# Attention and a softplus feed-forward: the first product of the last three token groups in seven block products

## The chip, the core and the metric

The kernel runs on one core of one Trainium2 chip. A core has five engines that run side by side, each through its own list of instructions in order: TensorE (PE in the profile; its weight loads are listed apart as PEld), VectorE (DVE), ScalarE (ACT), GpSimd (POOL) and SyncE (SP), which issues most transfers. They wait for each other through semaphores. TensorE writes its results to PSUM, eight banks of 128 partitions x 512 float32; VectorE and ScalarE read them from there. The metric is the device time of one execution in microseconds (us).

## The reference

Masked attention over 4 sequences of 768 tokens and 8 heads of 64, then a feed-forward layer without biases over all 3072 tokens:

```python
scores = scale * np.matmul(q, k.transpose(0, 1, 3, 2))
scores = np.where(keep, scores + bias, -1e9)      # 96 local keys and 8 global ones, linear bias by distance
a = softmax(scores)
x = np.matmul(a, v)                               # -> [3072, 512] after joining the heads
...
h = x @ w_in                                      # [512, 2048]
g = np.maximum(h, 0.0) + np.log1p(np.exp(-np.abs(h)))   # softplus
return g @ w_out                                  # [2048, 512]
```

## The kernel before

Tokens go in blocks of 128; two blocks make a group of 256, so there are 24 blocks (n = 0 to 23) and 12 groups (g = 0 to 11). A block's attention is: scores on TensorE (`sc`), bias added on VectorE (`z`), exponential on ScalarE (`ex`), the product with v on TensorE (`pv`, in two halves), the normalisation on VectorE (`nm`: a reciprocal and a multiplication), and a transpose by DMA (`xt`) into the group's tile XT. Copies of the global keys and values (`gk`, `gv`) and conversions to bf16 (`castq`, `castk`, `castv`) run on VectorE, ScalarE or POOL.

A group's first feed-forward product is eight steps `a g.p` (function `mm1`): each makes 256 rows of h for 256 tokens, with eight matmuls (4 parts of the 512 inputs x 2 blocks of rows; the weights are 128 x 128 of w_in, 256 columns of XT move), into one of two banks, h0 and h1. ScalarE then takes exp of the bank (`e g.p`, line 1075), and per two steps ln(1 + .) of 1024 columns (`ln g.i`, line 1086), which together are the softplus. The two `e` and one `ln` cover a quarter i of the 2048 rows.

The second product of the groups from 2 on is already done by a scheme with seven block products in place of eight (function `products`, steps `b g.j`, j = 1 to 7, eight matmuls of 256 columns each, line 521): sums of g are made beforehand (`ka g.j`, function `token_sums`, line 451), sums of w_out once (`ws`), and VectorE or ScalarE combines the products in the output tile (`oe g.*`, lines 482 to 504). For groups 2 to 9 products share banks in a chain (`CHAIN`), for 10 and 11 they have banks of their own. `st` stores a result.

What runs when is written out: the list `ORDER` holds every step with its engine (P, V, A, G for POOL, S), and the program issues the steps in just that order; so each engine's list is the part of `ORDER` with its letter. A step's dependences (class `Program`) only decide what it waits for. One instruction at the start loads ScalarE's function table with exp and ln (`table`, line 343).

## Time and profile before

| | |
|---|---|
| median of 3 runs | 210.53 us (209.85 to 210.83) |
| profiled execution | 210.08 us, of which the span from first to last instruction 208.3 us |
| granted TensorE clock | 0.997 of full speed |
| TensorE busy | 201.5 us (97%), 2211 matmuls |
| VectorE busy | 159.8 us (77%) |
| ScalarE busy | 169.0 us (81%) |
| POOL busy | 112.8 us (54%) |

A row of the profile names the line of the kernel, engine, operation, output <- inputs (buffer numbers left out), shapes and the number of instructions. In the view by groups the busy time, the mean duration of one in ns and the idle time ahead of them with its releasers follow; in the timeline a row begins with start and duration in us. A matmul's record runs until its result is drained, so records of following matmuls overlap; how far they really are apart is read from their starts.

### The profile page before, as it was taken

The page shows a single profiled execution, that of the slowest core. Times are in us where ns is not written, and L with a number is a line of the kernel's source. Part 1 is how long each engine was busy: PE and PEld are TensorE (multiplying, and loading weights), DVE is VectorE, ACT ScalarE, POOL GpSimd, SP SyncE. Part 2 cuts the span into 40 slices and gives each one's busy share as a digit, 9 for nine tenths or more (in the row PEclk, how much of TensorE's full clock was granted, in tenths as well). Part 3 has the DMA queues.
Part 4 walks back from the last instruction along what each step waited for, and adds up shares of the span by engine and source line. Part 5 has one row for each costly group of instructions (what it writes and reads, how often), then busy time and mean ns, then how long its engine had stood idle before and what let it go on. Part 6 is the DMA issues. An engine that isn't in the chain of part 4 may idle for free.

```text
span 208.3 us, 5515 instructions
## 1 busy us (share of the span) xinstructions
PE 201.5 (97%) x2211; PEld 164.8 (79%) x2211; DVE 159.8 (77%) x296; ACT 169.0 (81%) x240; POOL 112.8 (54%) x127
## 2 busy tenths in 40 slices
...
GB/s 175 364 361 388 387 358 361 332 245 249 201 271 214 257 210 312 172 188 296 195 212 259 191 200 221 145 152 102 106 73 62 92 5 142 63 0 0 104 22 181
DMA packets 70650, 40.99 MB, mean 197 GB/s; under 512 B 30433, under 2 KB 62689, under 8 KB 70625
## 3 DMA queue, kind: packets, MB, share of 16 engines
...
## 4 chain that ended last, share of the span: by engine, by line
PE 85%; DMA 8%; DVE 2%; POOL 2%; issue 1%; ACTq 0%; ACT 0%; POOLq 0%; DVEq 0%
PE h_ps L1060 38%; PE o_ps L521 25%; PE s_ps L950 5%; PE x_ps L1002 4%; PE s_ps L1107 3%; DMA raw<-in_q_dram 3%; DMA kT<-kb 3%; DMA XT<-xs 2%; PE x_ps L1235 2%; PE x_ps L521 2%; PE s_ps L521 1%; PE s_ps L810 1%; POOL vb L706 1%; PE o_ps L1107 1%; PE o_ps L1002 1%
## 5 line engine op out<-in xcount | busy, mean ns | idle before, releaser
L1060 PE MATMUL h_ps<-XT,w_in_bf 128*128 128x256 bf16 x768 | 94.4, 273 | 0.1
L1060 PEld LDWEIGHTS <-w_in_bf 128*128 128x128 bf16 x768 | 73.2, 98 | 11.0 <-DMA XT<-xs 0.3
L1075 ACT ACTIVATE e<-h_ps 128x512 f32<-128x512 f32 x96 | 60.1, 637 | 17.6 <-PE h_ps L1060 16.6
L1086 ACT ACTIVATE g<-e 128x1024 bf16<-128x1024 f32 x48 | 49.8, 1053 | 0.6
L976 DVE TENSOR_TENSOR z<-s_ps,biasA 128x1024 f32<-128x1024 f32 x38 | 45.9, 1218 | 3.5 <-PE s_ps L950 3.1
L983 ACT ACTIVATE pb<-z 128x1024 bf16<-128x1024 f32 (+1 forms) x44 | 43.4, 993 | 1.3 <-DVE z L976 0.6
L451 POOL TENSOR_TENSOR g<-g 128x1024 bf16<-128x1024 bf16 x11 | 23.9, 2171 | 23.7 <-DVE raw L451 23.5
L521 PEld LDWEIGHTS <-g 128*128 128x128 bf16 x320 | 30.9, 98 | 3.6
L451 POOL TENSOR_TENSOR raw<-g 128x1024 bf16<-128x1024 bf16 x9 | 19.6, 2177 | 15.0 <-ACT g L1086 13.5
L868 POOL COPY vb<-vb 4x512 bf16<-4x512 bf16 x22 | 14.9, 675 | 20.9 <-PE x_ps L1002 16.2
L706 POOL CAST vb<-raw 64x512 bf16<-64x512 f32 x32 | 21.6, 678 | 6.0 <-DMA raw<-in_v_dram 4.7
L521 PEld LDWEIGHTS <-raw 128*128 128x128 bf16 x240 | 22.6, 98 | 2.8
L521 PE MATMUL o_ps<-raw,raw 128*128 128x256 bf16 x192 | 24.3, 273 | 0.0
L451 DVE TENSOR_TENSOR raw<-g 128x1024 bf16<-128x1024 bf16 x21 | 17.2, 829 | 6.5 <-ACT g L1086 4.1
L521 PE MATMUL o_ps<-raw,g 128*128 128x256 bf16 x160 | 19.6, 273 | 0.0
L1002 PEld LDWEIGHTS <-pb 128*128 128x128 bf16 x352 | 16.4, 98 | 3.6 <-ACT pb L983 0.6
L1014 DVE TENSOR_TENSOR xs<-x_ps,rcp 128x256 bf16<-128x256 f32 x40 | 17.0, 424 | 1.4
L1002 PE MATMUL x_ps<-vb,pb 128*128 128x65 bf16 x304 | 15.8, 193 | 0.0
L521 PE MATMUL o_ps<-w_out_bf,g 128*128 128x256 bf16 x128 | 15.8, 273 | 0.0
L1235 PE MATMUL x_ps<-blank 128*128 128x512 bf16 x35 | 11.7, 454 | 1.2 <-DVE blank L1159 1.2
L1013 DVE RECIPROCAL rcp<-x_ps 128x4 f32<-128x4 f32 x40 | 7.1, 178 | 7.4 <-PE x_ps L1002 6.8
L674 POOL CAST qb<-raw 128x1024 bf16<-128x1024 f32 (+1 forms) x9 | 9.3, 1032 | 5.9 <-DMA raw<-in_q_dram 5.6
...
## 6 DMA issues: line engine op xcount, KB each, us to landing
...
```

What stands on the lines that cost most here:

```text
L451: (nc.vector if eng == "DVE" else nc.gpsimd).tensor_tensor(dst, a[0], b[0], ALU.subtract)
L521: nc.tensor.matmul(psum(j), lhs[:, f // 2, f % 2, :], w(f), start=(f == 0 and not (chain and j in "267")), stop=(f == 7), skip_group_check ...
L706: copy_on[eng](dst, src)
L868: copy_on[eng](vb_of(prev)[sl, :, 0:D], vb_of(first)[sl, :, 0:D])
L976: nc.vector.tensor_tensor(z, src, bias, ALU.add)
L983: nc.scalar.activation(pb[:, 0:nr, :].rearrange("p (y a) b -> p y (a b)", y=2), src, AF.Exp, scale=1.0 / root_d)
L1002: nc.tensor.matmul(xv[:, h, :], pb[:, 4 * (h % 2) + 2 * part + h // 2 if lone else u_all * (2 * (h % 2) + h // 2) + u, :], vb_of(prev if u ...
L1014: nc.vector.tensor_tensor(xs[:, 4 * part : 4 * part + 4, :], xv[:, :, 0:D], rcp[:][:, :, None].to_broadcast([P, 4, D]), ALU.mult,)
L1060: last = nc.tensor.matmul(hv[:, j, :], w_in_bf[:, m, fb * P : fb * P + P], XT[g % NXG][:, m, :], start=(m == 0), stop=(m == NM - 1),)
L1075: nc.scalar.activation(e[:, p % 2, :, :].rearrange("p j (b t r) -> p (j b) r t", b=2, r=2), hb[:].rearrange("p (a r t) -> p a r t", a=4, r=2),
L1086: nc.scalar.activation(gt[:, 2 * p - 2 : 2 * p + 2, :].rearrange("p a t -> p (a t)"), e[:].rearrange("p a j t -> p (a j t)"), AF.Ln, bias=1.0,
L1235: nc.tensor.matmul(x_ps[:], blank[:, 0:P], blank[:])
```

## The change

The first product of groups 9, 10 and 11 goes by seven block products as well (`mm1_seven`). Per quarter i of the rows there are four parts on TensorE, in one bank: `mA` (product 1, four matmuls), `mB` (3 and 4, eight), `mC` (5 and 2) and `mD` (7 and 6), each matmul with 128 x 128 weights and 128 columns moving, 28 in all. In between the bank is read: `my` copies product 1 out (ScalarE or VectorE), `mt` adds the two halves of the bank to the copy (VectorE, two instructions), `eo` takes the activation of half of the results straight from the bank (ScalarE), `md` subtracts the bank from the sum (VectorE), and `ed` takes the activation of that (ScalarE). The products 5, 2, 7 and 6 are accumulated onto what stands in the bank, so each part waits for the reading before it. Group 9 uses the banks h0 and h1 in turn; groups 10 and 11 use those and two more (t0, t1), halves of the two score tiles.

Sums of w_in are made once (`kw`, ten instructions of 1024 bf16 columns, six on VectorE and four on POOL), sums of x per group (`kx`, five of 256 columns, mostly on POOL). Group 9 keeps exp and ln (`eo`, `ed`, and `ln` over 1024 columns); groups 10 and 11 take softplus in one activation each, after one more table load, which follows the last `ln` of group 9. The outputs of groups 10 and 11 join the chain form, group 11 with single additions at the end. From the first `ln4.1` on the list `ORDER` is new; ahead of it it is the same. Six token sums `ka` more are on VectorE, and four more first copies of an output (`oe g.a`) are on ScalarE.

ScalarE's list around the first product of group 9, before (line 1075 is exp of a bank, 1086 ln, 983 the attention's exp, 855 and 868 copies of global keys and values):

```order
L1075 ACTIVATE e_104<-h_ps_64 128x4x2x64
L1086 ACTIVATE g_109<-e_106 128x1024
L1075 ACTIVATE e_105<-h_ps_64 128x4x2x64
L983 ACTIVATE pb_100<-z_94 128x1024
L855 COPY kT_88<-kTa_92 128x2x4x2 x2
L983 ACTIVATE pb_99<-z_96 128x1024
L868 COPY vb<-vb 4x8x64
L1075 ACTIVATE e_106<-h_ps_64 128x4x2x64
L1075 ACTIVATE e_104<-h_ps_65 128x4x2x64
L1086 ACTIVATE g_107<-e_104 128x1024
L983 ACTIVATE pb_97<-z_95 128x1024
L1075 ACTIVATE e_105<-h_ps_65 128x4x2x64
```

and now (1204 `my`, 1015 the attention's exp, 1181 `eo` and `ed`, 1267 and 1188 ln, 501 the first copy of an output):

```order
L1204 COPY raw_76<-h_ps_65 128x256
L1204 COPY raw_75<-h_ps_64 128x256
L1015 ACTIVATE pb_97<-z_95 128x1024
L1015 ACTIVATE pb_98<-z_96 128x1024
L887 COPY kT_89<-kTa_92 128x2x4x2 x2
L1181 ACTIVATE e_105<-h_ps_65 128x512
L1181 ACTIVATE e_104<-h_ps_64 128x512
L1267 ACTIVATE g_109<-e_106 128x1024
L1181 ACTIVATE e_105<-raw_76 128x512
L1204 COPY raw_76<-h_ps_65 128x256
L1188 ACTIVATE g_107<-e_105 128x1024
L501 COPY osb_111<-o_ps 128x512
```

Two exp and one ln per quarter became a copy, an exp from the bank, an exp from VectorE's result and an ln, so ScalarE's list now waits for VectorE inside a quarter.

VectorE's list at the same place, before (1013 and 1014 normalise, 976 adds the bias, 451 is a token sum, 485 to 498 combine outputs):

```order
L498 TENSOR_TENSOR osb_111<-osb_111,o_ps 128x2x256
L976 TENSOR_TENSOR z_96<-s_ps_62,biasA 128x1024
L1013 RECIPROCAL rcp_115<-x_ps 128x4
L1014 TENSOR_TENSOR xs_101<-x_ps,rcp_115 128x256
L451 TENSOR_TENSOR raw_79<-g_109 128x1024
L1013 RECIPROCAL rcp_112<-x_ps 128x4
L1014 TENSOR_TENSOR xs_102<-x_ps,rcp_112 128x256
L451 TENSOR_TENSOR g_109<-g_109 128x4x2x128
L485 TENSOR_TENSOR osb_110<-osb_110,o_ps 128x2x256
L976 TENSOR_TENSOR z_94<-s_ps_61,biasA 128x1024
L868 COPY vb<-vb 4x8x64 x2
L976 TENSOR_TENSOR z_95<-s_ps_62,biasA 128x1024
```

and now (1191 and 1192 are `mt`, 1195 `md`, 1204 `my`, 1045 and 1046 normalise, 470 is a token sum, 900 a copy of global values):

```order
L1191 TENSOR_TENSOR raw_76<-raw_76,h_ps_65 128x256
L1192 TENSOR_TENSOR raw_76<-raw_76,h_ps_65 128x256
L1191 TENSOR_TENSOR raw_75<-raw_75,h_ps_64 128x256
L1192 TENSOR_TENSOR raw_75<-raw_75,h_ps_64 128x256
L470 TENSOR_TENSOR raw_78<-g_108 128x1024
L1045 RECIPROCAL rcp_115<-x_ps 128x4
L1046 TENSOR_TENSOR xs_101<-x_ps,rcp_115 128x256
L1195 TENSOR_TENSOR raw_76<-raw_76,h_ps_65 128x512
L900 COPY vb<-vb 4x8x64
L470 TENSOR_TENSOR raw_78<-g_108 128x1024
L1195 TENSOR_TENSOR raw_75<-raw_75,h_ps_64 128x512
L1045 RECIPROCAL rcp_112<-x_ps 128x4
```

Between attention steps VectorE now has the two additions and the subtraction for each quarter, on which `mC`, `ed` and the next user of the bank wait.

ScalarE's list where the softplus of group 9 ends and that of group 10 begins, before (1075 exp of a bank, 1086 ln):

```order
L1086 ACTIVATE g_107<-e_104 128x1024
L1075 ACTIVATE e_106<-h_ps_65 128x4x2x64
L1075 ACTIVATE e_106<-h_ps_64 128x4x2x64
L1075 ACTIVATE e_104<-h_ps_65 128x4x2x64
L1075 ACTIVATE e_104<-h_ps_64 128x4x2x64
L1086 ACTIVATE g_108<-e_105 128x1024
L1075 ACTIVATE e_105<-h_ps_65 128x4x2x64
L1075 ACTIVATE e_105<-h_ps_64 128x4x2x64
L1086 ACTIVATE g_108<-e_106 128x1024
```

and now (359 is the table load, 501 the first copy of an output):

```order
L1188 ACTIVATE g_107<-e_106 128x1024
L1204 COPY e_106<-h_ps_65 128x256
L1181 ACTIVATE e_104<-raw_76 128x512
L1188 ACTIVATE g_107<-e_104 128x1024
L359 ACT_TABLE_LOAD
L501 COPY osb_110<-o_ps 128x512
L1181 ACTIVATE g_108<-h_ps_65 128x512
L1181 ACTIVATE g_108<-h_ps_64 128x512
L1181 ACTIVATE g_108<-s_ps_61 128x512
L1204 COPY e_105<-s_ps_62 128x256
L1181 ACTIVATE g_108<-e_105 128x512
L1181 ACTIVATE g_108<-e_104 128x512
```

From the table load on there is no ln; each half quarter is one activation from a bank (h_ps, s_ps) or from VectorE's result (e).

The diff, cut to its core (of the list `ORDER` one line that was taken out and two that came in):

```diff
     def in_order(self):
 
+        wants = [o for o in (self.ops[name] for name in self.placed) if o.table]
+        for o, p in zip(wants, wants[1:]):
+            if p.table != o.table:
+                o.then = p.table
...
-a8.6:P oe7.a:V gv20.0:G trq11:S castv11.00:V a8.7:P e8.6:A ka7.7:V ex20.0:A sc21.0:P trk11.1:S ka7.5:V b7.1:P e8.7:A
...
+kw6.0:G xt20:S pv21.0:P e8.7:A b6.7:P z22.1:V ln8.2:A st5.1.0:S mA9.0:P mA9.1:P b6.6:P kx9.7:G my9.1:A nm21.0:V
...
+my9.0:A ex22.0:A mB9.1:P ka7.2:G oe6.7:V mB9.0:P mt9.1:V ex22.1:A st6.1.0:S b7.3:P st6.0.0:S mt9.0:V mC9.1:P gk23:A
...
-CHAIN = range(FIRST_S, 10)
+CHAIN = range(FIRST_S, 12)
+APART = (11,)
 S_KEYS = {
-    10: {"3": ("o",), "4": ("o",), "5": ("x",), "2": ("x",), "1": ("s", 0, 0), "7": ("s", 1, 0), "6": ("s", 1, 0)},
-    11: {"3": ("o",), "4": ("o",), "5": ("x",), "2": ("x",), "1": ("s", 0, 0), "7": ("s", 1, 0), "6": ("h0",)},
+    11: {"3": ("x",), "4": ("x",), "1": ("s", 0, 0), "5": ("o",), "7": ("o",), "2": ("s", 1, 0), "6": ("s", 1, 0)},
 }
...
+EXP_TABLE, SOFT_TABLE = "natural_log_exp_and_others", "softplus"
+MM1S = (9, 10, 11)
+MM1_SOFT = (10, 11)
+SOFT = set()
...
+        if key[0][0] == "t":
+            return s_ps[int(key[0][1])][:, 1, :]
...
+        if g in MM1S:
+            view = g_t[g % NGB][:].rearrange("p a t -> p (a t)").rearrange("p (i q f t) -> p i q f t", i=4, q=4, f=2)
+            return view[:, :, {(1, 0): 0, (0, 1): 1, (0, 0): 2, (1, 1): 3}[tb, kh], :, :]
...
+                if g in APART:
+                    if j in "52":
+                        out_op(j, sub_one(j, "52".index(j)), [both["52".index(j)]], j, at + 1, 0.42)
+                    if j in "76":
+                        c = "76".index(j)
+                        out_op(j, add_one(j, c), [ok[c, c]], j, at + 1, 0.42)
+                    continue
...
+    WIN_SUM, b_homes, td_slots = {}, [], []
+
+    def win_part(F, K, h):
+        view = w_in_bf[:, 2 * K : 2 * K + 2, :].rearrange("p m (i k c) -> p m i k c", i=4, k=2)
+        return view[:, :, 2 * h : 2 * h + 2, F, :], [("win", 2 * i + K) for i in (2 * h, 2 * h + 1)]
+
+    def win_sums(rank):
+
+        slots = [idle.popleft() for _ in range(5)]
+        td_slots.extend(idle.popleft() for _ in range(2))
+        for z, (j, a, b, fn) in enumerate((
+            ("1", (0, 0), (1, 1), ALU.add),
+            ("5", (0, 0), (0, 1), ALU.add),
+            ("2", (1, 0), (1, 1), ALU.add),
+            ("7", (1, 1), (0, 1), ALU.subtract),
+            ("6", (0, 0), (1, 0), ALU.subtract),
+        )):
+            for h in range(2):
+                (x, xk), (y, yk) = win_part(*a, h), win_part(*b, h)
+                dst = raw_t[slots[z]].bitcast(BF16)[:, 1024 * h : 1024 * h + 1024]
+                dst = dst.rearrange("p (m i c) -> p m i c", m=2, i=2)
+                WIN_SUM[j, h] = dst
+
+                def ex(eng, dst=dst, x=x, y=y, fn=fn):
+                    (nc.vector if eng == "DVE" else nc.gpsimd).tensor_tensor(dst, x, y, fn)
+
+                op(f"kw{j}.{h}", "DVE", 0.0, rank, ex, reads=xk + yk, writes=[("WI", j, h)], port=True,
+                   after=users(("raw", slots[z], h)), alts={"DVE": 0.64, "POOL": 2.15})
+        for x in range(2):
+            for t, key in ((qb[x], "qb"), (kb[x], "kb")):
+                flat = t[:].rearrange("p a h d -> p (a h d)")
+                for part in range(4):
+                    b_homes.append((flat[:, W * part : W * part + W].rearrange("p (m t) -> p m t", m=2), (key, x, part)))
+
+    def mm1_seven(g, rank):
+        if not WIN_SUM:
+            win_sums(rank - 8.0)
+        B = {(kh, tb): XT[g % NXG][:, 2 * kh : 2 * kh + 2, P * tb : P * tb + P] for kh in range(2) for tb in range(2)}
+        bk = [("XT", 2 * (g % NXG) + tb) for tb in range(2)]
+        moving = {"2": (B[0, 0], bk[:1]), "5": (B[1, 1], bk[1:])}
+        for z, (j, a, b, fn) in enumerate((
+            ("3", (0, 1), (1, 1), ALU.subtract),
+            ("4", (1, 0), (0, 0), ALU.subtract),
+            ("1", (0, 0), (1, 1), ALU.add),
+            ("7", (1, 0), (1, 1), ALU.add),
+            ("6", (0, 0), (0, 1), ALU.add),
+        )):
+            dst, key = b_homes[(5 * (g - MM1S[0]) + z) % len(b_homes)]
+
+            def ex(eng, dst=dst, a=a, b=b, fn=fn):
+                (nc.vector if eng == "DVE" else nc.gpsimd).tensor_tensor(dst, B[a], B[b], fn)
+
+            op(f"kx{g}.{j}", "DVE", 0.0, rank, ex, reads=bk[a[1] : a[1] + 1] + bk[b[1] : b[1] + 1], writes=[key],
+               port=True, alts={"DVE": 0.25, "POOL": 0.6})
+            moving[j] = dst, [key]
+
+        def still(j, i):
+            if j in "34":
+                x, keys = win_part(*((0, 0) if j == "3" else (1, 1)), i // 2)
+                return x[:, :, i % 2, :], keys
+            return WIN_SUM[j, i // 2][:, :, i % 2, :], [("WI", j, i // 2)]
+
+        view = g_t[g % NGB][:].rearrange("p a t -> p (a t)").rearrange("p (i c) -> p i c", i=4)
+
+        for i in range(4):
+            n = 4 * (g - MM1S[0]) + i
+            soft = g in MM1_SOFT
+            ring_x = (("h0",), ("h1",), ("t0",), ("t1",)) if soft else (("h0",), ("h1",))
+            xkey = ring_x[n % len(ring_x)]
+            X = bank(xkey)
+            slot = n % NE
+            e = e_t[slot][:].rearrange("p a j t -> p (a j t)")
+            if soft:
+                td, tk, dk = e, ("e", slot, 0), ("e", slot, 1)
+            else:
+                z = td_slots[n % 2]
+                td, (tk, dk) = raw_t[z][:], raw_keys(z)
+            T, D_ = td[:, 0:W], td[:, 512:1024]
+            at = {j: X[:, 0:W] if j in "1357" else X[:, W:] for j in "1345276"}
+
+            def part(js, i=i, at=at):
+                def fn():
+                    for j in js:
+                        w, b = still(j, i)[0], moving[j][0]
+                        for f in range(2):
+                            for m in range(2):
+                                nc.tensor.matmul(
+                                    at[j][:, P * f : P * f + P], w[:, m, P * f : P * f + P], b[:, m, :],
+                                    start=f == m == 0 and j in "13", stop=m == 1, skip_group_check=True,
+                                )
+
+                return fn
+
+            def needs(js, i=i):
+                return sum((still(j, i)[1] + moving[j][1] for j in js), [])
+
+            def act(src, dst, fn, **kw):
+                def run():
+                    nc.scalar.activation(
+                        dst.rearrange("p (a t r) -> p a t r", a=4, r=2), src.rearrange("p (a r t) -> p a t r", a=4, r=2), fn
+                    )
+
+                return run
+
+            def log(i=i, e=e):
+                nc.scalar.activation(view[:, i, :], e, AF.Ln, bias=1.0)
+
+            def begin(X=X, T=T):
+                nc.vector.tensor_tensor(T, T, X[:, 0:W], ALU.add)
+                nc.vector.tensor_tensor(T, T, X[:, W:], ALU.add)
+
+            def end(X=X, T=T, D_=D_):
+                nc.vector.tensor_tensor(
+                    D_.rearrange("p (a c) -> p a c", a=2), T[:, None, :].to_broadcast([P, 2, W]),
+                    X.rearrange("p (a c) -> p a c", a=2), ALU.subtract,
+                )
+
+            first = users(("s", int(xkey[0][1]))) if xkey[0][0] == "t" and xkey not in pl.writer else []
+            r = rank + 4.0 * i
+            gk = {q: [("g", g % NGB, i, tb, kh) for tb, kh in c] for q, c in ((0, ((1, 0), (0, 1))), (1, ((0, 0), (1, 1))))}
+            op(f"mA{g}.{i}", "PE", 0.22, r, part("1"), reads=needs("1"), writes=[xkey], after=first, count=4)
+            op(f"my{g}.{i}", "ACT", 0.4, r + 0.3, lambda eng, X=X, T=T: copy_on[eng](T, X[:, 0:W]), reads=[xkey], writes=[tk],
+               alts={"ACT": 0.4, "DVE": 0.42})
+            op(f"mB{g}.{i}", "PE", 0.45, r + 0.6, part("34"), reads=needs("34"), writes=[xkey], count=8)
+            op(f"mt{g}.{i}", "DVE", 0.75, r + 0.8, begin, reads=[xkey], writes=[tk], count=2)
+            op(f"mC{g}.{i}", "PE", 0.45, r + 1.0, part("52"), reads=needs("52"), writes=[xkey], count=8)
+            outs = [view[:, i, 512 * q : 512 * q + 512] if soft else e[:, 512 * q : 512 * q + 512] for q in range(2)]
+            ok = [gk[q] if soft else [("e", slot, q)] for q in range(2)]
+            how = dict(table=SOFT_TABLE if soft else EXP_TABLE)
+            fn = AF.Softplus if soft else AF.Exp
+            op(f"eo{g}.{i}", "ACT", 0.64, r + 1.5, act(X, outs[0], fn), reads=[xkey], writes=ok[0], **how)
+            op(f"mD{g}.{i}", "PE", 0.45, r + 2.0, part("76"), reads=needs("76"), writes=[xkey], count=8)
+            op(f"md{g}.{i}", "DVE", 0.69, r + 2.5, end, reads=[xkey, tk], writes=[dk])
+            op(f"ed{g}.{i}", "ACT", 0.64, r + 3.2, act(D_, outs[1], fn), reads=[dk], writes=ok[1], **how)
+            if not soft:
+                op(f"ln{g}.{i}", "ACT", 0.99, r + 3.9, log, reads=ok[0] + ok[1], writes=gk[0] + gk[1], **how)
...
-            mm1(g, p, rank)
+            if g not in MM1S:
+                mm1(g, p, rank)
+        if g in MM1S:
+            mm1_seven(g, 16.0 * g)
...
+        if o.then:
+            table(o.then)
```

113 lines of the change are left out of this document (66 added, 47 removed).

## The prediction

> **What bounds the kernel now.** I read the page's busy times and the chain that ended last, then the busy times by stretch, then the instructions in order of time near the end.
>
> ```profile
> PE 201.5 (97%) x2211; PEld 164.8 (79%) x2211; DVE 159.8 (77%) x296; ACT 169.0 (81%) x240; POOL 112.8 (54%) x127
> ...
> PE 85%; DMA 8%; DVE 2%; POOL 2%; issue 1%; ACTq 0%; ACT 0%; POOLq 0%; DVEq 0%
> ```
>
> TensorE is busy 97% of the span and holds 85% of the chain. A busy PE could still be waiting inside a record, so the next view matters more (busy us of PE, PEld, DVE, ACT, POOL, then clock, DMA share, GB/s, for three stretches of 36 us).
>
> ```profile
> 30.00:66.00 36.00, 35.79 (x374) 25.06 (x372) 33.42 (x58) 34.12 (x47) 19.96 (x28) 1.00 1.16 267
> 113.00:149.00 36.00, 36.00 (x420) 31.81 (x417) 27.38 (x48) 31.35 (x45) 25.84 (x23) 1.00 0.86 170
> 149.00:185.00 36.00, 36.00 (x409) 31.78 (x407) 24.83 (x42) 29.62 (x43) 14.97 (x11) 1.00 0.26 67
> ```
>
> The second half, where the order is new, has no idle PE at all at full clock; VectorE stands at 76% and 69%, ScalarE at 87% and 82%. The timeline says the same in single steps:
>
> ```profile
> 187.05 1.91 PE L1060 MATMUL h_ps<-XT,w_in_bf 128*128 128x256 bf16 x16
> ...
> 188.79 1.91 PE L521 MATMUL o_ps<-raw,raw 128*128 128x256 bf16 x16
> ...
> 190.54 1.91 PE L1060 MATMUL h_ps<-XT,w_in_bf 128*128 128x256 bf16 x16
> ...
> 200.05 0.68 DVE L492 TENSOR_TENSOR osb<-osb,s_ps 128x512 f32<-128x512 f32 x1
> ...
> 200.65 0.68 DVE L482 COPY osb<-o_ps 128x512 f32<-128x512 f32 x1
> ...
> 203.68 1.04 PE L521 MATMUL h_ps<-raw,raw 128*128 128x256 bf16 x8
> 204.31 0.42 DVE L504 TENSOR_TENSOR osb<-osb,s_ps 128x256 f32<-128x256 f32 x1
> 204.75 0.42 DVE L504 TENSOR_TENSOR osb<-osb,h_ps 128x256 f32<-128x256 f32 x1
> ```
>
> Sixteen matmuls over 256 columns start 1.745 us before the next sixteen, 0.109 us each, whatever product they belong to. (VectorE's steps overlap a little when one follows the other: 200.05 to 200.65, 0.60 for a record of 0.68.) So the stage is worth what leaves TensorE's queue, less every wait that newly appears in it. Time saved on ScalarE alone is worth nothing here.
>
> **The change part by part.** *TensorE.* Each of the groups 9, 10, 11 loses 64 matmuls over 256 columns and gains 4 x 28 = 112 over 128 columns, each with its own weight load. Rows with that shape exist early in the kernel, and 65-column ones everywhere:
>
> ```profile
> 22.90 0.61 PE L810 MATMUL s_ps<-ident_p,qb 128*128 128x128 bf16 x8
> 23.35 0.61 PE L810 MATMUL s_ps<-ident_p,kb 128*128 128x128 bf16 x8
> 23.79 0.41 PE L1002 MATMUL o_ps<-vb,pb 128*128 128x65 bf16 x8
> ...
> 175.34 0.39 PEld L1002 LDWEIGHTS <-pb 128*128 128x128 bf16 x8
> 175.45 0.41 PE L1002 MATMUL x_ps<-vb,pb 128*128 128x65 bf16 x8
> 175.65 0.63 ACT L1075 ACTIVATE e<-h_ps 128x512 f32<-128x512 f32 x1 [0.23 <-PE h_ps L1060]
> ...
> 175.69 1.91 PE L1060 MATMUL h_ps<-XT,w_in_bf 128*128 128x256 bf16 x16
> ...
> 175.90 0.18 DVE L1013 RECIPROCAL rcp<-x_ps 128x4 f32<-128x4 f32 x1 [1.30 <-PE x_ps L1002]
> ```
>
> Sixteen of 128 columns take 23.79 - 22.90 = 0.89 us, 0.0556 each; eight of 65 columns with a full weight load each take 0.24 us, 0.03 each, so weight loads are hidden well below 128 columns. Removed: 192 x 0.109 = 20.9 us. Added: 336 x 0.0556 = 18.7 us. That is **-2.2 us**. The lower end is -2.5 (0.053, from 23.35 to 23.79 rounded down), the upper end is +11.9 (192 x 0.109 against 336 x 0.098, a weight load's record, if each load stood in the open); I take the 128-column row, which is the same shape.
>
> A rule of the Trainium skill speaks against this part: in "TensorE: Matmul & The Clock Gate", section "Back-to-back issue gap", a stream of load-and-multiply pairs is put at about 81 ns each at 128 columns. By that figure the added work would be 336 x 0.081 = 27.2 us and the sum of this part +6.3 us, an estimate from that page. The rows above disagree with it.
>
> *The new waits.* A block product's quarter passes one PSUM bank four times: product 1; a copy out (my); products 3 and 4; two additions (mt); 5 and 2; an activation (eo); 7 and 6; a subtraction (md). Each step needs the one before, through another engine. Durations (busy, mean ns):
>
> ```profile
> L1075 ACT ACTIVATE e<-h_ps 128x512 f32<-128x512 f32 x96 | 60.1, 637 | 17.6 <-PE h_ps L1060 16.6
> L1086 ACT ACTIVATE g<-e 128x1024 bf16<-128x1024 f32 x48 | 49.8, 1053 | 0.6
> ...
> L451 DVE TENSOR_TENSOR raw<-g 128x1024 bf16<-128x1024 bf16 x21 | 17.2, 829 | 6.5 <-ACT g L1086 4.1 <-PE o_ps L521 2.4
> L1014 DVE TENSOR_TENSOR xs<-x_ps,rcp 128x256 bf16<-128x256 f32 x40 | 17.0, 424 | 1.4
> ...
> L451 DVE TENSOR_TENSOR g<-g 128x1024 bf16<-128x1024 bf16 x9 | 6.2, 686 | 0.0
> ...
> L868 DVE COPY vb<-vb 4x512 bf16<-4x512 bf16 x7 | 3.5, 496 | 0.1
> L482 ACT COPY osb<-o_ps 128x512 f32<-128x512 f32 x5 | 2.9, 582 | 3.8 <-PE o_ps L521 3.8
> ...
> L492 DVE TENSOR_TENSOR osb<-osb,s_ps 128x512 f32<-128x512 f32 x2 | 1.4, 680 | 0.0
> L343 ACT ACT_TABLE_LOAD x1 | 1.3, 1283 | 1.5 <-PEq L1372 1.5
> ...
> L1211 ACT ACTIVATE biasA<-raw 128x256 bf16<-128x256 f32 x2 | 0.7, 408 | 0.0
> L488 DVE TENSOR_TENSOR osb<-osb,x_ps 128x256 f32<-128x256 f32 x2 | 0.8, 422 | 2.7 <-ACT osb L482 2.5 <-PE x_ps L521 0.2
> ```
>
> my is 0.4 (L1211, 256 columns); mt two of L488, 0.77 as they overlap; a bf16 sum (ka, kw) 0.69 (L451, g<-g), 0.6 behind another; eo 0.64; md 0.68 (L492). From PE taking up its next work to the reader's start there are 0.2 us (175.45 to 175.65 for ScalarE, 175.69 to 175.90 for VectorE). Back to PE it is 0.05; the row after that is a score product's step in the chain, 0.55:
>
> ```profile
> 14.61 1.09 ACT L817 COPY kTa<-s_ps 128x512 bf16<-128x512 bf16 x2
> ...
> 15.75 0.41 PE L950 MATMUL s_ps<-qT,kTa 64*128 64x128 bf16 x8 [0.48 <-ACT kTa L817]
> ```
>
> ```profile
> 150.98 0.55 PE s_ps L950 x16
> ```
>
> One round of a bank is then 28 x 0.056 + 0.4 + 0.77 + 0.64 + 0.68 + 4 x 0.25 = 5.1 us. Group 9 has two banks (h0, h1) and four quarters: 10.2 us at least. PE's queue from the first to the last part of group 9 holds 112 x 0.0556 + six output products of 0.87 + three value products of 0.24 + one score product of 0.55 (below) = 12.7 us, so the loop fits, but its margin has to hold what VectorE and ScalarE do between. Walking that place by the order: mD9.1 needs eo9.1, 0.2 + 0.64 + 0.05 = 0.89 after mC9.1, and behind mC9.1 stand pv21.1 and mC9.0, 0.69: a wait of 0.2. mA9.2 needs md9.0; VectorE has md9.1, gv22.1 (L868), ka7.7 and md9.0 from the end of mD9.1 on, 0.2 + 0.6 + 0.5 + 0.6 + 0.68 + 0.05 = 2.6 against sc23, mD9.0, mA9.3, pv22.0 and b7.4, 0.55 + 0.45 + 0.22 + 0.24 + 0.87 = 2.3: 0.3. mB9.2 needs my9.2 behind nm22.0: 0.1. Queued behind each on PE are the next output products, whose inputs are ready. **+0.6 us**; bounds 0 (the loop fits) and 2.5 (the margin 12.7 - 10.2 lost once). Groups 10 and 11 have four banks, since the score banks are free, and I put nothing there.
>
> *VectorE and ScalarE.* VectorE gains 12 pairs of additions (0.77), 12 subtractions (0.68), 6 sums of w_in and 6 token sums moved from POOL (0.69) and 3 copies (0.42): 9.2 + 8.2 + 8.3 + 1.3 = 27 us; it gives up some nine casts and evictions of 0.5 to 0.7, about 6: +21 us, most of it in the two stretches that now have 27.4 and 24.8 busy of 36. It would be near 97% there. ScalarE loses 24 exponentials and 8 logarithms (24 x 0.64 + 8 x 1.05 = 23.8) and gains 24 passes of 0.64, 9 copies of 0.4, 4 evictions of 0.58, 4 casts of about 0.6 and a table load of 1.28: 15.4 + 3.6 + 2.3 + 2.4 + 1.3 = 25, so it gains nothing; its work moves earlier. The stretch 30 to 66 shows the price of such a load: VectorE at 93%, ScalarE at 95%, PE short by 0.21 us. The other end is one collision with POOL:
>
> ```profile
> 175.83 2.12 POOL L451 TENSOR_TENSOR g<-g 128x1024 bf16<-128x1024 bf16 x1
> ...
> 176.45 2.04 DVE L451 TENSOR_TENSOR raw<-g 128x1024 bf16<-128x1024 bf16 x1
> ```
>
> There the 0.69 us VectorE step took 2.04, ending when POOL's did; where VectorE is full, all 1.35 us reach PE. I take **+0.5**, nearer the clean stretch, since such collisions lift the mean of 21 steps by 0.14 only (829 against 686).
>
> *Table load.* It stands behind ln9.3 and ahead of oe8.a, whose product's successor in the same bank (b8.1) has about 0.6 us to spare by the same walk: 0, or up to 0.7 if that cover goes. "ScalarE: Activation LUTs", section "What ACT_TABLE_LOAD costs", of the Trainium skill adds a drain of about 1.38 us to a load of 1.28; by that figure this term would be 0.8. The load's own 1283 ns agrees, no row shows the drain.
>
> *Softplus* has no row. Below: 0.64, like the exponential. Above: 0.64 + 0.53, an exponential and half a logarithm. I take 0.64, as exponential and logarithm cost alike per element; at the upper end 16 passes add 8.5 us to ScalarE where it is least loaded, and 0.5 to each bank round, some 1 us on PE.
>
> *Transposes by DMA, POOL, SP, the end.* x for group 11 now goes through one more sum (kx) before its first product.
>
> ```profile
> DMA to landing us min/median/max: 2.4/3.9/5.8
> ```
>
> From pv23.1: 0.2 + 0.6 + 3.9 + 0.25 + 0.05 = 5.0 us, against 5.3 us of PE work queued between: 0 at the median, 1.6 at the longest. POOL gains 4 sums of w_in and 12 small sums and gives up 6 of its 2.1 us token sums, about +2 us at 54% busy: 0. The last product, its 0.42 us addition and the store are as before: 0.
>
> Sum: -2.2 + 0.6 + 0.5 = **-1.1 us**. The profiled execution took 210.08 (span 208.3 and 1.8 around it) and would take 209.0; the median of the runs is 210.53, 0.45 above it, so I forecast **209.4**, own range 208.7 to 210.0.
>
> **The rivals.** *Gapless*: all waits stay covered, as PE's 36.00 of 36.00 shows for the order before. Against it: covers of 0.69 for chains of 0.89. -2.2: 208.3. *Waits eat it*: the loop in two banks also catches the queueing of a full VectorE, 1 to 1.5 us more: about 210.3. *Collisions* (the other side): VectorE full while POOL runs 2.1 us sums beside it. Two collisions beyond the 0.5 give +2.7 and end at 212.1; it decides from one and a half on (1.1 + 1.05 over 1.35). For it: VectorE full beside POOL's sums. Against: the small lift of that mean, though POOL ran less beside a full VectorE there. *Weight loads* (the change doesn't shorten TensorE): 128 columns don't cover a load when moving data and weights both change, by up to 98 ns each, 222.4 (+11.9); the skill's figure would give 216.8. Against it stand both rows above.
>
> **How the numbers follow.** A run can tell about 0.5%, 1.05 us. Forecast case 0.43 (three quarters of it below 209.5), gapless 0.13, waits eat it (a dear softplus among them) 0.25, collisions 0.15, weight loads 0.04. Faster: 0.32 + 0.13 = 0.45. Same: 0.11 + 0.25 = 0.36. Slower: 0.15 + 0.04 = 0.19. Range 208.0 (gapless at the -2.5 end) to 211.8, which leaves out the far part of the collisions and the last case.
>
> **What would show it.** The parts of group 9 to 11 in steps of 0.45 per eight matmuls; PE idle before mD9.1, mA9.2 and mB9.2 released by ScalarE or VectorE, 0.1 to 0.3 each; VectorE over 33 of 36 us in the second half; one table load of 1.28 with no PE idle behind it; eo and ed at 0.64. I am wrong if PE's idle in the second half is above 2 us, if eight matmuls of 128 columns take more than 0.5, or if VectorE's sums of bf16 show many records above 1 us.

## The result and the profile after

The changed kernel is slower: 213.0 us median (212.19 to 215.89), against 210.41 us (209.85 to 210.83) for the kernel before, timed in turn with it. The ratio is 1.0131, with an interval of 1.0103 to 1.0158. Here and below, ratios and their intervals leave out runs more than 1.5% above the fastest of the same kernel, while medians and ranges hold every run: left out are one of these six, two of four each of kw7d and x10, three of twelve of combo3, and one of twelve each of the second kw7v and of combo2 (260.06 us, at a granted clock of 0.755). Its profiled execution took 212.61 us, span 210.8. The page's busy times and its chain:

```profile
PE 201.2 (95%) x2355; PEld 165.0 (78%) x2355; DVE 181.5 (86%) x336; ACT 169.9 (81%) x248; POOL 119.6 (57%) x142
...
PE 83%; DVE 9%; ACT 2%; DMA 2%; issue 2%; DVEq 0%
```

VectorE has 21.7 us more work, as worked out, and its share of the chain went from 2% to 9%. The two stretches of 36 us:

```profile
113.00:149.00 36.00, 34.60 (x418) 29.86 (x413) 34.87 (x54) 33.34 (x47) 24.29 (x29) 1.00 0.92 184
149.00:185.00 36.00, 35.56 (x502) 32.44 (x502) 33.56 (x68) 28.66 (x44) 26.07 (x21) 1.00 0.22 67
```

TensorE, which had 36.00 of 36.00 in both, now idles 1.4 and 0.4 us there, and VectorE (third pair) stands at 97% and 93%. The parts of the new product run as fast as forecast: eight matmuls of 128 columns start 0.45 us before the next work.

```profile
172.55 0.61 PE L1169 MATMUL h_ps<-XT,raw 128*128 128x128 bf16 x8
173.00 0.41 PE L1034 MATMUL x_ps<-vb,pb 128*128 128x65 bf16 x8
```

The loss is in single waits of TensorE. All rows from 88 us on that carry one, in the timeline (idle time and what ended it in brackets):

```profile
102.48 0.62 PE L982 MATMUL s_ps<-qT,kT 64*128 64x128 bf16 x16 [0.52 <-DVE z L1008]
129.73 1.03 PE L546 MATMUL o_ps<-raw,raw 128*128 128x256 bf16 x8 [1.21 <-DVE osb L520]
149.05 0.40 PE L1034 MATMUL x_ps<-vb,pb 128*128 128x65 bf16 x8 [0.24 <-DVE xs L1046]
152.04 0.40 PE L1034 MATMUL x_ps<-vb,pb 128*128 128x65 bf16 x8 [0.18 <-DVE xs L1046]
197.32 1.91 PE L546 MATMUL o_ps<-w_out_bf,g 128*128 128x256 bf16 x16 [0.39 <-DVE osb L504]
```

By the order these are sc15.0, b5.7, pv20.1, pv21.0 and b10.5. (In the rows sc is L982, pv L1034, b L546, a L1229, mA to mD L1169, kw L1107, kx L1133, ka L470, oe L501 to L529, nm L1045 and L1046; kernels with a line put in have one more.) A matmul's record covers some of the wait that follows it; "late" below is measured from one matmul's start to the next, less the time of its columns, which gives some 0.15 us more for each and also shows shorter ones. What VectorE and POOL did ahead of the largest (rows of the other engines left out):

```profile
124.81 1.03 POOL L718 CAST kb<-raw 128x1024 bf16<-128x1024 f32 x1
125.56 2.92 DVE L1107 TENSOR_TENSOR raw<-w_in_bf 128x1024 bf16<-128x1024 bf16 x1 [0.27 <-ACT vb L738]
125.81 2.12 POOL L1107 TENSOR_TENSOR raw<-w_in_bf 128x1024 bf16<-128x1024 bf16 x1
128.12 1.26 POOL L718 CAST kb<-raw 128x1024 bf16<-128x1024 f32 x1 [0.19 <-DMA raw<-in_k_dram]
128.40 0.68 DVE L1008 TENSOR_TENSOR z<-s_ps,bias 128x512 f32<-128x512 f32 x1
129.00 0.67 DVE L520 TENSOR_TENSOR osb<-osb,o_ps 128x512 f32<-128x512 f32 x1
```

The sum of weights kw7.0 needs 0.69 us alone. Here it took 2.92, until 128.48, 0.55 us after POOL's kw7.1 had ended (127.93). Behind it in VectorE's list stand z18.1 (L1008) and oe5.c (L520), and b5.7 waits for oe5.c. sc15.0 is the same with ka4.1 beside two casts on POOL (2.09 us, until 101.30), pv20.1 and pv21.0 with kw2.0 (1.55) and ka6.2 (1.19), a few steps ahead in VectorE's list, which has no idle time there.

From a3.1 (65 us, where the new order has not begun to matter) to the end, the kernel before took 143.4 us without any wait and this execution 145.9 with 4.5 us of lateness: collisions 3.0, the loop of group 9 0.9, b10.5 and b10.7 0.6. Without them it would be 141.4, so TensorE's saving of 2.0 us is there and more than twice as much is lost.

### The profile page after: what moved, and what is told of

Its sections match the earlier page's. It is cut to its first block, busy times and chain, and to the rows that moved or that the text cites. A ratio compares the mean times of both kernels' runs of the same rounds, so it can differ in the third digit from the quotient of the medians.

```text
span 210.8 us, 5897 instructions
## 1 busy us (share of the span) xinstructions
PE 201.2 (95%) x2355; PEld 165.0 (78%) x2355; DVE 181.5 (86%) x336; ACT 169.9 (81%) x248; POOL 119.6 (57%) x142
## 4 chain that ended last, share of the span: by engine, by line
PE 83%; DVE 9%; ACT 2%; DMA 2%; issue 2%; DVEq 0%
PE h_ps L1229 26%; PE o_ps L546 25%; PE h_ps L1169 6%; PE s_ps L982 5%; PE x_ps L1034 4%; PE o_ps L1288 3%; PE s_ps L1288 3%; PE s_ps L1169 3%; DMA raw<-in_q_dram 2%; PE x_ps L1416 2%; DVE z L1008 2%; DVE raw L1107 2%; DVE raw L470 2%; PE s_ps L546 1%; PE s_ps L842 1%
## 5 line engine op out<-in xcount | busy, mean ns | idle before, releaser
L1229 PE MATMUL h_ps<-XT,w_in_bf 128*128 128x256 bf16 x576 | 71.3, 273 | 0.0
L1229 PEld LDWEIGHTS <-w_in_bf 128*128 128x128 bf16 x576 | 54.3, 98 | 8.9 <-issue 0.2
L1257 ACT ACTIVATE e<-h_ps 128x512 f32<-128x512 f32 x72 | 44.6, 636 | 5.3 <-PE h_ps L1229 4.6
L1008 DVE TENSOR_TENSOR z<-s_ps,biasA 128x1024 f32<-128x1024 f32 x38 | 45.4, 1215 | 1.0 <-PE s_ps L982 0.8
L1267 ACT ACTIVATE g<-e 128x1024 bf16<-128x1024 f32 x36 | 37.6, 1054 | 0.4
L546 PEld LDWEIGHTS <-g 128*128 128x128 bf16 x320 | 30.7, 98 | 4.1 <-issue 0.5
L546 PE MATMUL o_ps<-raw,raw 128*128 128x256 bf16 x224 | 28.4, 272 | 1.2 <-DVE osb L520 1.2
L546 PEld LDWEIGHTS <-raw 128*128 128x128 bf16 x240 | 22.7, 98 | 3.8 <-issue 1.4
L470 POOL TENSOR_TENSOR raw<-g 128x1024 bf16<-128x1024 bf16 x7 | 15.0, 2139 | 8.8 <-ACT g L1181 4.3
L1034 PEld LDWEIGHTS <-pb 128*128 128x128 bf16 x352 | 16.0, 97 | 4.5 <-issue 0.8
L546 PE MATMUL o_ps<-w_out_bf,g 128*128 128x256 bf16 x152 | 18.4, 273 | 0.4 <-DVE osb L504 0.4
L470 DVE TENSOR_TENSOR raw<-g 128x1024 bf16<-128x1024 bf16 x23 | 17.9, 790 | 1.0 <-ACT g L1267 0.6
L470 POOL TENSOR_TENSOR g<-g 128x1024 bf16<-128x1024 bf16 x7 | 15.2, 2172 | 6.2 <-DVE raw L470 6.1
L1046 DVE TENSOR_TENSOR xs<-x_ps,rcp 128x256 bf16<-128x256 f32 x40 | 17.0, 424 | 1.4
L546 PE MATMUL o_ps<-raw,g 128*128 128x256 bf16 x144 | 17.5, 272 | 0.0
L1034 PE MATMUL x_ps<-vb,pb 128*128 128x65 bf16 x304 | 15.9, 193 | 0.4 <-DVE xs L1046 0.4
L1169 PEld LDWEIGHTS <-raw 128*128 128x128 bf16 x240 | 14.9, 98 | 1.1 <-issue 0.5
```

The source lines that it names most:

```text
L470: (nc.vector if eng == "DVE" else nc.gpsimd).tensor_tensor(dst, a[0], b[0], ALU.subtract)
L546: nc.tensor.matmul(psum(j), lhs[:, f // 2, f % 2, :], w(f), start=(f == 0 and not (chain and j in ("67" if g in APART else "267"))), stop= ...
L1008: nc.vector.tensor_tensor(z, src, bias, ALU.add)
L1034: nc.tensor.matmul(xv[:, h, :], pb[:, 4 * (h % 2) + 2 * part + h // 2 if lone else u_all * (2 * (h % 2) + h // 2) + u, :], vb_of(prev if u ...
L1046: nc.vector.tensor_tensor(xs[:, 4 * part : 4 * part + 4, :], xv[:, :, 0:D], rcp[:][:, :, None].to_broadcast([P, 4, D]), ALU.mult,)
L1169: nc.tensor.matmul(at[j][:, P * f : P * f + P], w[:, m, P * f : P * f + P], b[:, m, :], start=f == m == 0 and j in "13", stop=m == 1, skip ...
```

## Experiments

Two theories. *Collisions*: sums in bf16 on VectorE that meet POOL's instructions stretch, and the step behind them is late. *Load*: VectorE (and ScalarE) are simply full between 105 and 165 us, so any step more there costs its time. All kernels below are the changed kernel with the edit shown, those called combo with the edits of the ones before them as the text says; soft and soft2 are the kernel before with an edit.

**One collision away (kw7v).** The other half of the same sum goes from POOL to VectorE, which gets 0.69 us more to do.

```diff
-kw7.0:V sc18.0:P trk11.0:S kw7.1:G
+kw7.0:V sc18.0:P trk11.0:S kw7.1:V
```

> The changed kernel with one letter new: the second half of the w_in sum kw7 goes to VectorE, behind the first half, and no longer to POOL beside it. In the changed kernel's trace the first half took 2.92 us in place of 0.69, ending 0.55 us after POOL's sum, and TensorE then idled 1.37 us ahead of b5.7. Collision theory (a VectorE bf16 sum cannot run while POOL is at work): both halves take 0.6 to 0.9 us, the idle time ahead of b5.7 falls below 0.3, the kernel is 1.0 to 1.4 us faster than the changed one, about 211.8. Load theory (VectorE simply has too much to do): it has 0.7 us more in that place, the idle time stays at 1.4 or grows to 2, the time stays at 213 or rises to 213.7.

210.81 us median, ratio to the kernel before 1.0011 (0.9983 to 1.0039): 2.2 us less than the change as it was, by more work on the fullest engine, and more than the 1.0 to 1.4 expected: in its trace the waits at pv20.1 and pv21.0 are gone together with that at b5.7. VectorE's rows there, two sums in 1.42 us and oe5.c 0.76 us earlier, though this execution was by then 0.8 us behind the other:

```profile
126.27 1.42 DVE L1107 TENSOR_TENSOR raw<-w_in_bf 128x1024 bf16<-128x1024 bf16 x2 [0.27 <-ACT vb L738]
127.64 0.69 DVE L1008 TENSOR_TENSOR z<-s_ps,bias 128x512 f32<-128x512 f32 x1
128.24 0.68 DVE L520 TENSOR_TENSOR osb<-osb,o_ps 128x512 f32<-128x512 f32 x1
```

The load theory has the wrong sign. (The profiled execution was the slowest of ten, 212.7 us; transposes by DMA were late in it, of which more below.)

**The collision put back, without work for VectorE (kw7d).** To kw7v, a needless POOL sum is added at the old place (the half sum kw1.0 written a second time, same values).

```diff
-kw7.0:V sc18.0:P
+kw7.0:V kd1.0:G sc18.0:P
```

> kw7v, which runs as fast as the kernel before, plus one needless POOL sum of 2.1 us (a second write of the half sum kw1.0, same values) at the place where kw7.1 stood on POOL. VectorE's order and work are those of kw7v. Collision theory: kw7.0 or kw7.1 on VectorE stretches to some 2.7 us or more, b5.7 waits 1 to 2.4 us again, the time is 1 to 2.4 us above kw7v, ratio to the kernel before 1.005 to 1.012. Load theory: POOL has idle time there and VectorE does nothing more, so the time is that of kw7v, ratio 1.000 to 1.003.

Ratio 1.0118 (1.0061 to 1.0174); the four runs took 211.78 to 215.72 us. The loss is back, and in the profiled execution (215.0 us) larger than expected: VectorE's two sums now take 4.91 us, POOL's cast coming straight behind its sum, and b5.7 waits 3.2 us.

```profile
125.50 4.91 DVE L1107 TENSOR_TENSOR raw<-w_in_bf 128x1024 bf16<-128x1024 bf16 x2 [0.27 <-ACT vb L738]
...
125.74 2.12 POOL L1107 TENSOR_TENSOR raw<-w_in_bf 128x1024 bf16<-128x1024 bf16 x1
127.81 1.03 POOL L718 CAST kb<-raw 128x1024 bf16<-128x1024 f32 x1
...
131.66 1.03 PE L546 MATMUL o_ps<-raw,raw 128*128 128x256 bf16 x8 [3.21 <-DVE osb L520]
```

**The collision left, another step behind it (kw7late).**

```diff
-kw7.0:V sc18.0:P trk11.0:S kw7.1:G e7.0:A pv17.0:P z18.1:V a7.1:P ex17.1:A oe5.c:V
+sc18.0:P trk11.0:S kw7.1:G e7.0:A pv17.0:P z18.1:V a7.1:P ex17.1:A oe5.c:V kw7.0:V
```

> The changed kernel with one name moved: kw7.0 stands behind oe5.c on VectorE and not ahead of it. The same work on the same engines. Collision theory: oe5.c is in time and b5.7 does not wait for it; kw7.0 now meets the end of kw7.1 and castk10.0 on POOL and pushes back nm17.0, so some 0.3 to 0.9 us of wait comes at pv17.1; the time falls by 0.5 to 1.5 us against the changed kernel, ratio to the kernel before 1.006 to 1.011. If the wait ahead of b5.7 is not on the path, the time stays at 1.013.

211.97 us, ratio 1.0084 (1.0051 to 1.0117). b5.7 starts without a wait; kw7.0 still takes 1.73 us, and now the normalisation behind it makes pv17.1 wait 0.67:

```profile
127.41 0.68 DVE L520 TENSOR_TENSOR osb<-osb,o_ps 128x512 f32<-128x512 f32 x1
...
128.00 1.73 DVE L1107 TENSOR_TENSOR raw<-w_in_bf 128x1024 bf16<-128x1024 bf16 x1
128.15 1.03 POOL L718 CAST kb<-raw 128x1024 bf16<-128x1024 f32 x1
...
128.62 1.04 PE L546 MATMUL o_ps<-raw,raw 128*128 128x256 bf16 x8
...
130.33 0.40 PE L1034 MATMUL x_ps<-vb,pb 128*128 128x65 bf16 x8 [0.67 <-DVE xs L1046]
```

So what a collision costs depends on who stands behind it.

**Parts of the change alone.** x10 gives product 1 of group 10 (b10.1) the bank x; plain9 has the old product in group 9 and the seven only in 10 and 11; oldmm has the new order with the old product everywhere, no kw or kx, and one softplus per half block in groups 10 and 11.

```diff
 S_KEYS = {
+    10: {"1": ("x",)},
```

> The changed kernel with product 1 of group 10's second feed-forward product in bank x in place of bank o. In the changed kernel TensorE idled 0.55 us ahead of b10.5, which had to wait for the addition oe10.1 to read bank o: 0.2 + 0.69 + 0.05 = 0.94 us after b10.1, with 0.45 us of work between. If that hand-over is the cause, the idle time ahead of b10.5 goes and the kernel is 0.5 us faster than the changed one, about 212.5. If the end is bound by something behind it (VectorE's chain from ed11.3 on, POOL's ka10.5), another step idles in its place and the time stays within 0.15 us.

```diff
-MM1S = (9, 10, 11)
+MM1S = (10, 11)
```

> Seven block products for groups 10 and 11 alone; group 9's first product goes by eight steps of eight matmuls over 256 columns again, at the places where its parts stood, with exp and ln. The w_in sums and the rest of the new order stay. Sum theory (streamed time, plus each idle time in the trace): TensorE streams 0.7 us more, the loop's idle times ahead of mD9.1, mA9.3, mA9.2, b7.5 (0.2 + 0.27 + 0.22 + 0.13) and some before them go, 0.8 to 1.2: 0.1 to 0.5 us faster than the changed kernel, about 212.7. If the two-bank loop were the main cause of the loss, it would be 2 us faster, about 211.

```diff
-MM1S = (9, 10, 11)
+MM1S = ()
-SOFT = set()
+SOFT = {(g, i) for g in (10, 11) for i in range(4)}
```

> The new order with the old first product in all groups (eight steps of 256 columns at the places of the parts, spread evenly), no w_in sums, no x sums; softplus in one pass in groups 10 and 11. It shows what the moved steps cost by themselves. Collision theory: the idle time ahead of sc15.0 (0.6 us, behind the token sum ka4.1 that took 2.09 beside POOL's casts) stays, that ahead of b5.7 (1.37) goes with the w_in sums, and in the stretch from 85 to 150 us TensorE idles 1 us more than in the kernel before: 211 to 211.7 in all. If the new order of the older steps were the main cause, it would stay at 212.5 to 213.

x10: ratio 1.0129 (1.0043 to 1.0215); the wait ahead of b10.5 is gone, but with so wide an interval its time says nothing. plain9: 1.0168 (1.0112 to 1.0223); without group 9's loop it is no faster, because b5.7 is 2.36 us late there and a step of group 7 (b7.1) 0.9 by the place that I gave group 9's logarithms. oldmm: 1.0406 (1.0338 to 1.0473); b5.7 is in time, without kw7, but six other steps are 0.6 to 2.3 us late (a8.1, b7.1, a10.1, b8.1, b10.1, b10.5), most of them behind ScalarE, which I put down to my placing of the old steps. Neither of the last two measures what it was made for: a part can't be taken out of an order written for the whole.

**Softplus and the table (soft, soft2).** The kernel before, in its own order, with one softplus per half block in groups 10 and 11 and without their logarithms; in soft2 ln9.3 is moved ahead of the first softplus.

```diff
-SOFT = set()
+SOFT = {(g, i) for g in (10, 11) for i in range(4)}
```

> The order of the kernel before, with the old product, and in groups 10 and 11 one softplus per half block in place of the exponential, its logarithm gone (8 logarithms of about 1.06 us less on ScalarE, one load of the function table more). By the prediction's terms TensorE bounds those groups and the time does not move: ratio 0.998 to 1.002. If ScalarE's logarithms were on the path there, up to 1 us faster, 0.995; if the table load is on it, 1.3 us slower, 1.006.

```diff
-e9.7:A gv23.0:V
+e9.7:A ln9.3:A gv23.0:V
-e10.1:A ln9.3:A pv23.0:P
+e10.1:A pv23.0:P
```

> soft with one name moved: the last logarithm of group 9 (ln9.3) ahead of the first softplus, so that ScalarE loads its function table once there and not three times (softplus, back to exponential and logarithm, softplus). The trace of soft shows 2.4 and 0.4 us of wait on TensorE behind the two loads of 1.28 us around ln9.3. If these loads were the whole loss of soft (3.6 us), soft2 is within 0.5% of the kernel before, 0.5 to 1.2 us above it for the one load and ln9.3 ahead of e10.0: ratio 1.002 to 1.006. If softplus itself costs the time (0.74 us here for a half block, 0.64 for an exponential), it stays above 1.010.

soft: 214.07 us, ratio 1.0164 (1.0126 to 1.0202). I had overlooked that ln9.3 stands behind the first softplus in the old order, so the table changes three times:

```profile
171.18 1.28 ACT L354 ACT_TABLE_LOAD   x1
172.47 1.34 ACT L1239 ACTIVATE g<-h_ps 128x512 bf16<-128x512 f32 x2
173.83 1.28 ACT L354 ACT_TABLE_LOAD   x1
175.12 1.06 ACT L1262 ACTIVATE g<-e 128x1024 bf16<-128x1024 f32 x1
176.20 1.28 ACT L354 ACT_TABLE_LOAD   x1
...
178.28 3.48 PE L1224 MATMUL h_ps<-XT,w_in_bf 128*128 128x256 bf16 x16 [2.27 <-ACT g L1239]
```

The last row shows a second loss: sixteen matmuls that take 1.91 us elsewhere took 3.48. From 178.1 to 181.6 us TensorE's granted clock was 0.50, which cost some 1.7 us (an estimate, half of that time). With the waits at a10.5 (2.44) and a10.3 (0.36) that makes 4.5, against the 4.4 by which this execution was longer than the kernel before from a3.1 on (147.8 and 143.4). More on that clock below.

soft2: 211.66 us, ratio 1.0055 (1.0040 to 1.0071), 1.09 us over the kernel before; its one new wait, 1.06 late at a10.3 behind ln9.3 and the load, is all of it. Softplus itself costs nothing, and it saves nothing where TensorE is the bound. In the changed kernel the one load (172.04 us) has no waiting matmul behind it.

**All known waits away (combo, combo2, kw7v once more).** combo is kw7v, x10's bank, and ka4.1 moved behind ka4.7, where POOL's run of casts is over. combo2 also puts another step ahead of three waiting ones in group 9's loop (sc23.0, b7.4, mB9.3).

```diff
-b3.6:P castv9.10:A ka4.1:V castk8.0:G
+b3.6:P castv9.10:A castk8.0:G
-ka4.6:V ldq9:S a5.7:P ka4.7:V
+ka4.6:V ldq9:S a5.7:P ka4.7:V ka4.1:V
```

> The changed kernel with three edits: the half sum kw7.1 moved from POOL to VectorE (as in kw7v), the sum ka4.1 on VectorE moved behind z15.0, ka4.6 and ka4.7, where POOL has run out of its casts, and product 1 of group 10 (b10.1) into the bank x. Collision theory: the waits ahead of sc15.0 (0.68 us, some 0.1 left), of b5.7 (1.4 to 2.4) and of b10.5 (0.55) are gone from the trace, and the time is 1.1 us below kw7v, about 209.6, ratio to the kernel before 0.994 to 0.997. If the sums' collisions and the one bank were not the cause but the sheer load of VectorE, which does as much as in kw7v here, the time stays at that of kw7v, ratio 1.000 to 1.003.

```diff
-mC9.0:P gv22.0:G nm21.1:V mD9.1:P eo9.0:A sc23.0:P
+mC9.0:P sc23.0:P gv22.0:G nm21.1:V mD9.1:P eo9.0:A
-mD9.0:P gv22.1:V ka7.7:V ed9.1:A mA9.3:P pv22.0:P b7.4:P
+mD9.0:P b7.4:P gv22.1:V ka7.7:V ed9.1:A mA9.3:P pv22.0:P
-mA9.2:P mB9.3:P
+mB9.3:P mA9.2:P
```

> The three edits of combo (kw7.1 to VectorE, ka4.1 behind ka4.7, b10.1 into the bank x) and three exchanges in TensorE's order in the loop of group 9, so that something stands between a block product and the step that frees its bank: sc23.0 ahead of mD9.1, b7.4 ahead of mA9.3, mB9.3 ahead of mA9.2. The profile of combo shows 0.2, 0.3 and 0.2 us of wait at these three. If they are on the path, they go and the time is 0.7 us below combo: profiled execution about 209.0, median 209.3 to 210.0, ratio to the kernel before 0.994 to 0.998. If VectorE's load is what holds the loop, the waits come back at the next steps and the time stays at 1.001.

> kw7v once more, beside combo2 on one chip, since combo and kw7v were timed on two. By the traces combo2 saves the waits at sc15.0 (0.7), b10.5 (0.55) and in the loop (0.7), so kw7v should be 1.5 to 2 us above it; by the medians of combo and kw7v (210.7 and 210.8), no more than 0.8.

combo: 210.70 us (209.54 to 212.43), ratio 1.0014 (0.9989 to 1.0040). Its profiled execution took 209.7 and has neither sc15.0's, b5.7's nor b10.5's wait; its median is that of kw7v all the same, so the collision theory's 1.1 us are not in the times. combo2: 211.12 us, ratio 1.0035 (1.0013 to 1.0056), no gain: the waits in the loop came back at the next steps (mB9.3 0.5, pv22.1 0.3), so there the load of VectorE and ScalarE does hold. kw7v once more: 1.0026 (1.0000 to 1.0053); ka4.1 took 0.69 us in its profiled execution and sc15.0 did not wait, though nothing was changed there, but mA11.1 was 1.05 late, for the last transposed x. The executions differ from each other by more than these edits.

**What differs between executions.** combo3 is combo without two waits for XT: xt13 is issued ahead of a store, mA11.1 stands behind b8.7. Then the changed kernel and combo3 were each profiled twice more.

```diff
-nm13.1:V sc15.0:P gv14.1:V st3.0.0:S
+nm13.1:V xt13:S sc15.0:P gv14.1:V st3.0.0:S
-mA11.1:P mB10.3:P kx11.7:G md10.2:V b8.7:P
+mB10.3:P kx11.7:G md10.2:V b8.7:P mA11.1:P
```

> The three edits of combo and two more, at waits for the transposed x (XT) that the traces of the others show: xt13 ahead of st3.0.0 in SP's queue (a6.1 waited 0.4 to 0.5 us for it in combo, combo2, kw7d, kw7late and the second kw7v), and mA11.1, which needs the sum kx11.1 of the last XT, behind b8.7 (it was 1.05 to 1.09 us late in kw7late and the second kw7v, 0 in others). If the late transposes make the spread of combo (209.5 to 212.4), the median falls to its low end, 209.3 to 209.9, ratio to the kernel before 0.994 to 0.998, and no run is above 211. If VectorE's and ScalarE's full load between 105 and 165 us makes it, the median stays at 210.5 or above with the same spread.

> The changed kernel once more, for its trace: its executions lie between 212.2 and 215.9 us and only one of them, at 212.6, has been seen in detail. If the spread comes from collisions on VectorE and from late transposes that are there in one execution and not in the next, the difference of two executions from 65 us to the end equals the difference of their listed waits on TensorE to 0.3 us, and the same few places (sc15.0, b5.7, a6.1, pv20.1, mA11.1) change size. If it is a general slowing, the steps themselves last longer and the waits stay.

> As after_2: a third execution of the changed kernel, same expectations.

> combo3 once more, for its trace: its seen execution took 209.2 us with 1.0 us of waits on TensorE, others took up to 212.3. By collisions and late transposes: an execution near 211 or above shows 1 to 3 us more of waits behind stretched sums on VectorE or late XT, qT or kT. By a general slowing: the same 1.0 us of waits and longer steps.

> As combo3_2: a third execution of combo3, same expectations.

combo3: 210.91 us (208.64 to 212.25), ratio 0.9989 (0.9962 to 1.0016); the medians alone give 1.0008. The expected 209.3 to 209.9, with no run above 211, did not come, so these two waits were not what spread the runs. TensorE's lateness by cause in seven profiled executions, in us, from a3.1 to the end (combo4 is below):

| | after | after_2 | after_3 | combo3 | combo3_2 | combo3_3 | combo4 |
|---|---|---|---|---|---|---|---|
| whole execution | 212.6 | 213.6 | 216.6 | 209.2 | 211.1 | 212.4 | 209.3 |
| collisions (sc15.0 with b4.3, b5.7, pv20.1, pv21.0) | 3.0 | 3.1 | 3.9 | 0 | 0 | 0 | 0 |
| transposes (XT, qT; mA11.1, b8.7 by kx11.1) | 0 | 0.4 | 1.3 | 0.1 | 1.2 | 4.1 | 0.3 |
| loop of group 9 | 0.9 | 0.9 | 0.9 | 0.8 | 0.8 | 0.8 | 0.8 |
| b10.5, b10.7 | 0.6 | 0.6 | 0.6 | 0.1 | 0.1 | 0.1 | 0.1 |
| unassigned | 0 | 0 | 0.7 | 0 | 0 | 0 | 0 |
| a3.1 to the end | 145.9 | 146.5 | 149.7 | 142.1 | 143.3 | 145.8 | 142.7 |
| less all lateness | 141.4 | 141.5 | 142.4 | 141.1 | 141.2 | 140.8 | 141.5 |

(The 1.0 us at a8.1 in combo3_2 stand under the transposes although the profile names a ScalarE copy (gv20.1), which stands behind a8.1 in `ORDER`, so that a8.1 can't wait for it: the last ScalarE step ahead of it, e7.6, had ended 0.66 us before, and XT landed 0.13 us before it.) The last row lies within 0.7 us in six of seven, 1.9 to 2.6 us below the 143.4 of the kernel before. after_3 stands 1 us above the others because its clock was halved for a while. From 132.4 us on, 1.3 us after the late b5.7 had started, it had (TensorE, its weight loads, VectorE, ScalarE, POOL, then granted clock, DMA share, GB/s):

```profile
132.40:135.80 3.40, 3.40 (x32) 2.33 (x31) 2.20 (x7) 3.08 (x4) 3.18 (x2) 0.50 0.57 114
```

Matmuls of 256 columns started 0.21 us apart there in place of 0.109, which costs some 1.7 us (an estimate, half of the 3.4): most of the 0.7 "unassigned" and the 1.0 in the last row. With it, all seven lie within about 0.7. So the loss is waits at named places and, in this one execution, the clock behind the largest of them; it is not a general slowing. b5.7's share of the collisions was 1.4 us in the first execution and 2.3 in the other two, where POOL's cast came straight behind its sum and kw7.0 lasted 3.89 us:

```profile
125.56 3.89 DVE L1107 TENSOR_TENSOR raw<-w_in_bf 128x1024 bf16<-128x1024 bf16 x1 [0.27 <-ACT vb L738]
...
125.81 2.12 POOL L1107 TENSOR_TENSOR raw<-w_in_bf 128x1024 bf16<-128x1024 bf16 x1
127.88 1.03 POOL L718 CAST kb<-raw 128x1024 bf16<-128x1024 f32 x1
```

and combo3's third execution (212.4 us) waits for transposes by DMA:

```profile
125.28 1.03 PE L1230 MATMUL h_ps<-XT,w_in_bf 128*128 128x256 bf16 x8 [0.86 <-DMA XT<-xs]
139.16 0.23 PE L983 MATMUL s_ps<-qT,kT 64*128 64x128 bf16 x2 [0.93 <-DMA qT<-qb]
140.00 1.91 PE L1230 MATMUL h_ps<-XT,w_in_bf 128*128 128x256 bf16 x16 [0.21 <-DMA XT<-xs]
150.33 0.62 PE L983 MATMUL s_ps<-qT,kT 64*128 64x128 bf16 x16 [0.29 <-DMA qT<-qb]
179.79 1.03 PE L547 MATMUL o_ps<-raw,raw 128*128 128x256 bf16 x8 [0.95 <-DVE osb L521]
```

The new order issues some of them late: xt15 was issued 4.2 us ahead of a7.0 in the kernel before (118.06 and 122.27) and 3.0 ahead in the changed one (122.10 and 125.06), with its data ready 6 us earlier (nm15.1 ended at 115.97) and SP's list held up at other transfers.

**The transposes moved up (combo4, xtonly).** combo4 is combo3 with xt14 to xt18 where their data is ready, and kx11.1 behind md10.2; xtonly has these moves, with xt13's and mA11.1's, and nothing else.

```diff
-ldk11:S
+ldk11:S xt14:S
-trk9.1:S
+trk9.1:S xt15:S
-nm16.1:V
+nm16.1:V xt16:S
-nm17.1:V
+nm17.1:V xt17:S
-trk10.1:S
+trk10.1:S xt18:S
-md10.2:V
+md10.2:V kx11.1:V
```

> combo3, and the transposes of x moved up in SP's queue to where their data is ready: xt14 behind ldk11 (it was ready at 110.1 us and issued at 119.4), xt15 behind trk9.1, xt16 behind ldq10, xt17 ahead of trq10, xt18 ahead of st5.0.0; kx11.1 behind md10.2 on VectorE, so that oe8.c does not stand behind it. The three traces of combo3 differ by 0, 1.0 and 3.3 us of waits for late XT and qT. If SP's order is what lets them come late, the waits at a7.0, a8.1 and b8.7 are gone, the upper runs of combo3 (212) go, and the median falls from 210.9 to 209.3 to 209.9, ratio to the kernel before 0.994 to 0.997. If the transposes come late for another reason (the time from issue to landing itself), the median stays near 210.9 and the spread at 3 us.

> The changed kernel with the order of SP's transposes of x, of kx11.1 and of mA11.1 from combo4, and nothing else: the collisions stay. By collisions as the first cause and late transposes as the second: b5.7 still waits 1.4 to 2.4 us, the time is 212.0 to 212.6, some 0.5 to 1 below the changed kernel, its upper runs (214 to 216) gone. If the late transposes were the first cause, it is near 210.8.

combo4: 210.45 us (209.33 to 211.08), ratio 0.9997 (0.9982 to 1.0012). The spread fell from combo3's 3.6 to 1.8 us, the kernel before having 1.1 beside it, and its profiled execution shows no wait for a7.0, a8.1 or b8.7; but the median did not fall to the expected 209.3 to 209.9. By the medians it stands at 1.0003 and combo3 at 1.0008, which is no difference. combo3's runs above 211.1 are gone, as expected, and so is its lowest. xtonly: 211.62 us, ratio 1.0069 (1.0042 to 1.0096): 1.4 us better than the changed kernel, more than expected. Its gain is not the transposes' alone: b5.7 didn't wait in the profiled execution, the steps around it having shifted, and qT was late there instead (0.99 and 0.42 us). So the repair of one collision takes away nearly all of the loss (1.0011), that of the transposes about half (1.0069, b5.7's wait gone with it), both together all of it. combo4's profiled execution, the shortest of its twelve, is 0.75 us shorter than the profiled one of the kernel before (209.33 against 210.08), but its median is not; what the slower ones wait for stays open, and no version here is measurably faster than the kernel before.

## Why the prediction was wrong

*TensorE, -2.2 us*: right. The table's last row gives -1.9 to -2.6, and a matmul of 128 columns takes 56 ns at the median of 408 from start to start. The 81 ns of the Trainium skill ("TensorE: Matmul & The Clock Gate", "Back-to-back issue gap") are not what this stream shows. (The lower end of that term, -2.5, belongs to 0.055 us a matmul; with the 0.053 that stands there it would be -3.1.)

*The two-bank loop of group 9, +0.6*: right in kind, 0.9 in size: mD9.1 0.20, mA9.2 0.22, mA9.3 0.27, b7.5 0.13, b7.3 0.08. The walk had 0.2 and 0.3 for the first two, 0.1 for mB9.2, which did not wait, and nothing for the other three. combo2's other order of TensorE did not win it back.

*VectorE and ScalarE, +0.5, "nearer the clean stretch" than one collision*: this is the step that failed. It was 3.0 to 3.9 us, at three or four places, and kw7v, kw7d and kw7late show for the largest, b5.7, that it is a collision and not load. At sc15.0 the executions show it in which ka4.1 took 0.69 us and nothing waited (after_2, the second kw7v); pv20.1 and pv21.0 are put down to it by the traces alone. Two errors are in it. I read the price of a collision from one row where VectorE started inside a single POOL sum (2.04 us, 1.35 too long) and made that its size; POOL's next instruction can follow without a gap, and then VectorE waits for both (2.92, 3.89). And I weighed how often collisions come by a mean over 21 steps (829 against 686 ns) in an order where little stood close behind those steps. That mean told of the old order's places. The change puts six sums of w_in on VectorE and four on POOL and moves POOL's casts; kw7.0 and kw7.1 stand in `ORDER` with no other step of these two engines between them, and that could have been read there. The rival "collisions", given 0.15, is the case that came, with its mechanism. Its 212.1 is 0.9 below the measured 213.0: 0.6 of that is b10.5 and b10.7, 0.3 the loop.

*Table load, 0, and softplus, 0.64*: right for the load, near for the softplus. The passes, by groups:

```profile
L1181 ACT ACTIVATE g<-e 128x512 bf16<-128x512 f32 x8 | 5.9, 746 | 1.6 <-DVE e L1195 1.4
L1181 ACT ACTIVATE e<-raw 128x512 f32<-128x512 f32 x4 | 3.0, 752 | 0.4 <-DVE raw L1195 0.3
L1181 ACT ACTIVATE g<-s_ps 128x512 bf16<-128x512 f32 x4 | 2.4, 599 | 5.0 <-PE s_ps L1169 5.0
```

The softplus takes 0.60 us from PSUM and 0.75 from SBUF, and the exponential from SBUF (second row) the same 0.75. (In soft and soft2 a softplus from PSUM took 0.74 beside an exponential of 0.64; why it is not 0.60 there is open.) The drain of 1.38 us that the Trainium skill ("ScalarE: Activation LUTs", "What ACT_TABLE_LOAD costs") adds to a load is not seen here: in soft the next activation starts 0.01 us after each load, and the load 0.02 after the activation ahead of it.

*Transposes, 0 at the median*: right for the first execution, wrong as a rule. The prediction worked out one place (kx11.1: 5.0 us of chain against 5.3 of cover); it was 1.0 to 1.1 us late in four executions of kernels with that order (kw7v once more, kw7late, after_3, x10). The others, a6.1, a7.0, a8.1 and the score products, it left out; SP's list sets when their transposes start. POOL's term was wrong as well: +2 us was forecast and it has 6.8 more (119.6 against 112.8), beside the sums of VectorE that it holds up.

*Groups 10 and 11 and the end, 0*: a miss of 0.6. b10.5 takes the bank that oe10.1 must have read, and only mD11.3 (0.45) stands between against a chain of 0.2 + 0.69 + 0.05. x10 and combo show it gone with another bank. I had walked the banks of the new product and not those of the old one that moved.

My three terms beside the saving, 0.6 + 0.5 + 0, were in truth 0.9 + 3.0 + 0.6 in the profiled execution, and up to 1.3 more for transposes and 1.7 for the clock in others.
